# Seven block products for a third group of a dense layer, and steps of an attention moved around it

## The chip, the cores and the metric

The kernel runs on one core of one Trainium2 chip. The metric is device time in microseconds (us), measured several times; the kernel before has a median of 198.84 us. The five engines of the core work side by side and wait for each other through semaphores: TensorE (matmuls; PE in the profile, PEld for its weight loads), VectorE (DVE), ScalarE (ACT), GpSimd (POOL) and SyncE (SP), whose queue issues nearly all DMAs here. Each engine works through its own instructions in the order in which they were recorded. Matmul results lie in PSUM, eight banks of 128 x 512 fp32; everything else lies in SBUF.

## The reference

A linear attention with decay, in blocks of 64 tokens (batch 4, 8 heads, 768 tokens, head size 64), whose output goes into a dense layer, a gelu and a second dense layer (3072 tokens, 512 -> 2048 -> 512):

```python
for b in range(nb):
    qb, kb, vb = (q[:, :, sl], k[:, :, sl], v[:, :, sl])
    intra = np.einsum('bhic,bhjc->bhij', qb, kb) * Dmask[None]
    intra = np.einsum('bhij,bhjd->bhid', intra, vb)
    inter = np.einsum('bhid,bhde->bhie', qb * lam_pow[None], kv_state)
    out[:, :, sl] = intra + inter
    kb_dec = kb * rev_pow[None]
    kv_state = lam_block * kv_state + np.einsum('bhsd,bhse->bhde', kb_dec, vb)
x = attn_out.transpose(0, 2, 1, 3).reshape(B * S, H * D)
h = x @ w_in
g = 0.5 * h * (1.0 + np.tanh(c * (h + 0.044715 * h * h * h)))
return g @ w_out
```

## The kernel before

**Attention.** It is cut into 24 steps. Step n holds 256 tokens and 4 of the 8 heads; steps 2i and 2i + 1 make token block i. What a step needs: three loads of 256 KB (`load_step`, L60), the casts to fp16 (`cast_q` on VectorE, L282; `cast_k` on ScalarE, L295), a transpose of q and k by DMA on SyncE's queue (`transpose_dma`, L303, from step 8 on), the scaling of v on GpSimd (`scale_v`, L266), the scores (L350), their mask on VectorE (`causal`, L360), the key-value products (L385 or L450), the outputs (L399 and L408, or L436 and L461), the copy of the outputs into xT on ScalarE (`x_out`, L487), and twice the running state on VectorE (`update`, t at L503 and L506) with its spreading on GpSimd (u, L513). `R(n, s)` (L902) does scores of step n and outputs of step s; `burst(ns, ss)` (L415) does the same for two steps at once. `U(n)` is the second state update. `prep(s)` is casts, transpose and v, and also issues the loads of step s + 3.

**Dense layers.** The twelve token blocks make seven groups: `groups = [[0, 1], [2], [3], [4, 5], [6, 7], [8, 9], [10, 11]]`. When the last output of a group is copied, `queue_group(g)` (L544) puts the group's matmul pieces into a list, `filler`, and `fill(n)` (L898) takes the next n pieces from it, between the attention steps. The order on TensorE is therefore written out by hand, from L1060 on for the steps 13 to 23. Each piece is a closure that records its matmuls and what follows them on the other engines.

**First product, plain** (`mm1`, L557): for a group of 512 tokens 16 pieces of 4 matmuls of 512 columns (L561), each followed by a gelu on ScalarE (L565). Groups 0 to 4 use it.

**First product, by blocks** (`seven`, L726): groups 5 and 6, named in `SEVEN` (L531). The 2 x 2 block product over half the inner size, half the hidden size and half the tokens is done with seven products instead of eight, from four sums of blocks of w_in (`sum_win`, L144, on VectorE, made once, in tiles `ws`) and four sums of blocks of x (`sum_x`, L713, tiles `xs`). The hidden size is cut into four sets k. In a set each of the products m = 1 to 7 has 4 matmuls of 256 columns (L739), into banks X (two, in turn), W and Y. Product 1 opens X and is copied to SBUF by ScalarE (`copied("m1")`), 6 is added in the same bank and copied by VectorE (`"u2"`), 7 is added to that, then 4. Product 2 goes to W and VectorE adds the copy of 1. Product 5 opens Y and is copied by ScalarE (`"q"`), 3 is added in the same bank. VectorE adds the copies to the banks (`added`, L760), ScalarE then does the four gelus of the set (L756). The copies lie in tiles of the pool `ld`, which also holds the loads of q and k.

`merge` (L781) puts these pieces between the second product's pieces of the group before, which are still in `filler`: this is a mixed stretch. `SLOTS` says after which m one of the old pieces follows, `lead` how many old pieces stay in front of the mixed ones.

**Second product** (`product`, L616): for groups 1 to 6 also seven block products (m, and p for a half of the rows), with sums of w_out blocks made once and sums of the gelu output (`sum_g`, L602, tiles `gs`, VectorE). ScalarE copies (L657), VectorE adds (L677, L683, L686), and for the last quarter GpSimd (L692). `behind` hangs a `sum_g` on a piece. A group in front of one in `SEVEN` cuts its pieces in two halves.

Of the kernel before, what the change touches and what calls it, by code (L numbers as in the profile page):

```python
# [8 lines left out]
FP32 = mybir.dt.float32  # L9
FP16 = mybir.dt.float16  # L10
AF = mybir.ActivationFunctionType
ALU = mybir.AluOpType
# [3 lines left out]
def kernel(  # L16
# [10 lines left out]
    nc = tc.nc  # L27
# [32 lines left out]
    def load_step(s, names="qkv"):  # L60
        b, r = divmod(s, 2 * NSB)
        sb, half = divmod(r, 2)
        ts = ld32.setdefault(s, [])
        for nm, src in (("q", q), ("k", k), ("v", v)):
            if nm not in names:
                continue
            t = ld.tile([P, HH, 2, D], FP32, tag=nm + "32", name=f"{nm}32_{s}")
            rows = src[b, half * HH : (half + 1) * HH, sb * SB : (sb + 1) * SB, :]
            queue = nc.scalar if (nm, s) == ("v", 0) else nc.sync
            pin(queue.dma_start(out=t[:].rearrange("p h j d -> p h (j d)"),  # L70
                                in_=rows.rearrange("h (p j) d -> p h (j d)", j=2)))
            ts.append(t)
# [172 lines left out]
    def prep(s):  # L245
        prep_qk(s)
        prep_v(s)
# [21 lines left out]
    def prep_qk(s):  # L269
        cast_qk(s)  # L270
        transpose_dma(s)

    def cast_qk(s):
        cast_q(s)
        cast_k(s)
# [252 lines left out]
                                for i in range(2)]  # L528
        return gs_kept[1:]

    SEVEN = (5, 6)  # L531
    SLOTS = {5: {1: 0, 2: 1, 5: 1, 6: 1, 3: 1, 7: 1}, 4: {1: 0, 2: 1, 5: 0, 6: 1, 3: 1, 7: 1}}
    groups = [[0, 1], [2], [3], [4, 5], [6, 7], [8, 9], [10, 11]]
    group_of = {sb: (g, i) for g, sbs in enumerate(groups) for i, sb in enumerate(sbs)}
    filler = []
# [8 lines left out]
    def queue_group(g, lead=0, per_set=0):  # L544
# [177 lines left out]
        def release():  # L722
            while pending:
                pending.pop(0)()

        def seven(m, k):  # L726

            st = of_set.setdefault(k, {})
            for name in {1: "X", 2: "W", 5: "Y"}.get(m, ""):
                key = name + str(k % 2) if name == "X" else name  # L730
                if key not in hbank:
                    hbank[key] = ps_M.tile([P, 2, SB], FP32, tag="M", name="H" + name)
                st[name] = hbank[key]
            dst = st[{2: "W", 5: "Y", 3: "Y"}.get(m, "X")]
            a, b = X_FACTORS[m]
            for i in range(2):
                f = 2 * k + i
                for c in range(2):
                    pin(nc.tensor.matmul(  # L739
                        dst[:, i, :],  # L740
                        w_in_block(a, slice(c, c + 1), slice(f * P, f * P + P))[:, 0],
                        x_block(b, slice(c, c + 1))[:, 0],
                        start=(m in (1, 2, 5) and c == 0 and i == 0), stop=(m in (2, 3, 4) and c == 1),
                        skip_group_check=True))

            def copied(name, tag, eng):
                t = ld.tile([P, HH, 2, D], FP32, tag=tag, name=f"{name}_{g}_{k}")
                t = t[:].rearrange("p h j d -> p (h j d)").rearrange("p (i t) -> p i t", i=2)
                if eng is nc.scalar:
                    pin(nc.scalar.activation(out=t, in_=dst[:], func=AF.Copy))  # L750
                else:
                    pin(eng.tensor_copy(out=t, in_=dst[:]))
                st[name] = t

            def gelu(F, T, src):
                pin(nc.scalar.activation(out=gT[:, 2 * k : 2 * k + 2, F, T * SB : T * SB + SB],  # L756
                                         in_=src, func=AF.Gelu_apprx_tanh))

            def added(F, T, name):
                pin(nc.vector.tensor_tensor(st[name], dst[:], st[name], ALU.add))  # L760
                pending.append(lambda src=st[name]: gelu(F, T, src))

            if m == 1:
                copied("m1", "q32", nc.scalar)
            elif m == 2:
                added(0, 0, "m1")
            elif m == 5:
                copied("q", "q32", nc.scalar)
                release()
            elif m == 6:  # L770
                copied("u2", "k32", nc.vector)
            elif m == 3:
                added(0, 1, "u2")
            elif m == 7:
                added(1, 1, "q")
            elif m == 4:
                pending.insert(0, lambda: gelu(1, 0, dst[:]))
            if k == HF // 2 - 1 and m in (3, 7, 4):
                release()

        def merge(lead, per_set):  # L781

            old = filler[:]
            del filler[:]

            def h(n=1):
                for _ in range(min(n, len(old))):
                    filler.append(old.pop(0))

# [12 lines left out]
            h(lead + len(old) + 1 - 28 - 1 if len(old) >= 28 else lead - 1)  # L802
            sums = [1, 2, 4, 3]
            unread = {1: 16, 2: 12, 4: 8, 3: 4}
            slots = SLOTS[per_set]
            for k in range(HF // 2):
                for m in (1, 2, 5, 6, 3, 7):
                    filler.append(lambda m=m, k=k: seven(m, k))
                    if m == 2 and k > 0:
                        filler.append(lambda k=k: seven(4, k - 1))  # L810
                    while k >= 2 and sums and m == 7 and len(old) <= unread[sums[0]]:
                        also(sum_g, 0, 4, (sums.pop(0),))
                        if len(sums) == 2 and k == 2:
# [51 lines left out]
        if g in SEVEN:  # L865
            merge(lead, per_set)
            parts = (0, 1) if g + 1 in SEVEN else (None,)
            for m, p in order:
                for part in parts:
                    filler.append(lambda m=m, p=p, part=part: product(m, p, part))  # L870
            at = len(filler) - len(order) * len(parts)
            for k, m in enumerate((2, 4, 3)):
                behind(len(parts) * k, 4, 8, (m,))
            return
        for i in range(HF):
            for fs in ([[i, i + HF]] if per == 2 else [[i], [i + HF]]):
# [21 lines left out]
    def fill(n):  # L898
        for _ in range(min(n, len(filler))):
            filler.pop(0)()  # L900

    def R(n, s, ahead=None, keep=False):  # L902

        if n is not None:
            scores(n)
        if ahead:
            ahead()
        products(n, s)
        if n is not None:
            causal(n)  # L910
        if s is not None and s % 2 == 1:
            g, i = group_of[s // 2]
            if i == len(groups[g]) - 1 and g > 0:
                queue_group(g)
        if n is not None and not keep:
            update(n, 0)

    def U(n):
        update(n, 1)
# [138 lines left out]
            sum_win((n - 7) // 2, (n - 1) % 2, nc.vector)  # L1058

    cast_qk(16)  # L1060
    load_step(17, "qk")
    transpose_dma(16)
    load_step(17, "v")
# [13 lines left out]
    fill(1)  # L1077
    U(15)
    U(16)
    fill(8)  # L1080
    prep(18)
    R(17, 15)
    fill(1)
    U(17)
    fill(1)
    sum_win(3, 0, nc.vector)
    fill(2)
    prep(19)
    sum_win(3, 1, nc.vector)
    fill(2)  # L1090
    sum_win(4, 0, nc.vector)
    fill(2)
    sum_win(4, 1, nc.vector)
    fill(2)
    prep_qk(20)
    fill(1)
    prep_qk(21)
    prep_v(20)
    fill(3)

    burst((18, 19), (16, 17))
    prep_v(21)
    fill(2)
    U(18)
    U(19)
    fill(4)
    prep_qk(22)
    fill(2)
    burst((20, 21), (18, 19), 11, 4)
    fill(3)  # L1110
    U(20)
    U(21)
    fill(20)
# [39 lines left out]
```

## Time and profile before

| | |
|---|---|
| median of 3 runs | 198.84 us (198.83 to 198.92) |
| span of the profiled execution, first to last instruction | 197.1 us; a time of its own is not listed for it |
| TensorE busy | 191.5 us, granted clock 1.000 over the span |
| VectorE, ScalarE, GpSimd busy | 151.6, 122.2, 73.3 us |
| DMA moved | 38.13 MB, 193 GB/s in the mean |

Where the last groups stand on TensorE in the profiled execution (us from the start of the span):

| stretch | what TensorE does |
|---|---|
| 87.1 to 95.2 | burst of steps 13 and 14, first product of group 3, burst of 15 and 16 |
| 95.2 to 98.7 | rest of group 3's first product |
| 98.7 to 111.9 | group 3's second product, with step 17 at 103.1 |
| 111.9 to 129.2 | group 4's plain first product, with bursts of 18, 19 and of 20, 21 |
| 129.2 to 153.9 | group 4's second product, mixed with group 5's first from 134.0 |
| 153.9 to 160.3 | burst of 22, 23, last outputs |
| 160.3 to 181.4 | group 5's second product, mixed with group 6's first from 161.6 |
| 181.4 to 193.8 | group 6's second product |

How to read it: a row of the timeline has the start, the duration of the (merged) instructions, the engine, the line of the kernel, the operation, the output and inputs by name, the shape and the count; in brackets stands the idle time before it with what ended it. Durations of matmuls are modelled and overlap, so the pitch from start to start is used for them. The page's slices cut the span into 40 parts of 4.9 us; a digit is the busy share in tenths.

### The profile page before, as it was taken

How to read it: one execution, taken by the hardware profiler on the slowest of the kernel's cores; microseconds unless marked ns; L12 is line 12 of the kernel's file. 1: busy time of each engine (PE TensorE's matmuls, PEld its weight loads, DVE VectorE, ACT ScalarE, POOL GpSimd, SP SyncE). 2: the span in 40 equal slices, each digit the busy share in tenths (PEclk: the TensorE clock that was granted, in tenths of full speed). 3: DMA queues.
4: the chain of work that ended last, by engine and by line, in shares of the span. 5: the costliest groups of instructions: out<-in, count | busy, mean ns of one | idle time of the engine just before them, and what ended most of it. 6: DMA issues, size and time to landing. Idle time of an engine off the chain costs nothing.

```text
span 197.1 us, 5915 instructions
## 1 busy us (share of the span) xinstructions
PE 191.5 (97%) x2431; PEld 140.0 (71%) x2431; DVE 151.6 (77%) x297; ACT 122.2 (62%) x249; POOL 73.3 (37%) x85
## 2 busy tenths in 40 slices
PE   8979999999999999999999999999999999999993
PEld 2556544446888888654688764588888888888882
DVE  4797622789999889849999937998668996588620
ACT  3673878357874685686835378844768845779221
POOL 6594123456554841068854517165002030002000
PEclk9999999999999999999999999999999999999999
DMA  6999999999999999999997998400220300030205
GB/s 172 290 324 384 387 387 388 299 287 292 236 216 225 259 343 220 213 266 247 271 268 149 268 328 213 88 4 0 53 85 25 109 6 0 0 110 0 106 19 197
DMA packets 62810, 38.13 MB, mean 193 GB/s; under 512 B 18624, under 2 KB 55744, under 8 KB 62784
## 3 DMA queue, kind: packets, MB, share of 16 engines
q1 hardware_dynamic: 62240, 37.50, 75.0%
q8 instruction: 19, 0.31, 0.6%
q10 hardware_dynamic: 544, 0.26, 0.5%
q14 instruction: 7, 0.06, 0.1%
HBM read 27.26 MB, written 6.29 MB: 170 GB/s over the span
## 4 chain that ended last, share of the span: by engine, by line
PE 89%; SPq 4%; DMA 4%; ACT 0%; issue 0%
PE Hps L561 25%; PE MX L640 18%; PE MY L640 9%; PE HX L739 7%; PE O2ps L576 7%; PE MW L640 4%; DMA wi<-in_moe_w_in_dram 4%; SPq L70 4%; PE HY L739 4%; PE S L350 3%; PE Hps L830 3%; PE HW L739 2%; PE OK L408 2%; PE O L461 1%; PE O L436 1%; PE OK L399 1%
## 5 line engine op out<-in xcount | busy, mean ns | idle before, releaser
L561 PE MATMUL Hps<-xT,w_in 128*128 128x512 f16 (+1 forms) x288 | 50.5, 332 | 0.0
L513 POOL TENSOR_TENSOR u<-t,lumask 128x256 f16<-128x256 f32 x40 | 30.9, 787 | 39.5 <-DVE t L506 25.8
L561 PEld LDWEIGHTS <-w_in 128*128 128x128 f16 x288 | 27.9, 98 | 19.1
L565 ACT ACTIVATE gT<-Hps 128x512 f16<-128x512 f32 x56 | 33.3, 597 | 11.3 <-PE Hps L561 10.8
L360 DVE TENSOR_TENSOR PT<-S,mask 128x512 f16<-128x512 f32 x48 | 30.3, 681 | 7.5 <-PE S L350 7.5
L266 POOL TENSOR_TENSOR v<-v,dv 128x512 f16<-128x512 f32 x24 | 27.7, 1156 | 18.2 <-DMA v<-in_v_dram 14.2
L640 PEld LDWEIGHTS <-gs 128*128 128x128 f16 x320 | 31.2, 98 | 3.6
L640 PEld LDWEIGHTS <-gT 128*128 128x128 f16 x240 | 23.3, 98 | 3.2 <-ACT gT L565 0.2
L640 PE MATMUL MX<-w_sum,gs 128*128 128x256 f16 x160 | 21.4, 273 | 0.0
L282 DVE TENSOR_TENSOR qk<-q,dq 128x512 f16<-128x512 f32 x23 | 18.4, 802 | 1.7 <-DMA q<-in_q_dram 1.7
L692 POOL TENSOR_TENSOR o<-u,q 128x512 f32<-128x512 f32 (+1 forms) x5 | 6.3, 1253 | 35.2 <-ACT u L657 35.2
L295 ACT ACTIVATE qk<-k 128x512 f16<-128x512 f32 x23 | 14.4, 625 | 7.4 <-DMA k<-in_k_dram 7.2
L610 DVE TENSOR_TENSOR gs<-gT 128x1024 f16<-128x1024 f16 (+1 forms) x24 | 16.9, 711 | 1.6 <-ACT gT L565 1.6
L576 PE MATMUL O2ps<-w_out,gT 128*128 128x512 f16 x64 | 14.6, 379 | 0.0
L487 ACT ACTIVATE xT<-OK 128x256 f16<-128x256 f32 x26 | 9.9, 452 | 6.7 <-PE OK L408 6.2
L739 PEld LDWEIGHTS <-ws 128*128 128x128 f16 x128 | 12.5, 97 | 1.8
L657 ACT ACTIVATE u<-MX 128x256 f32<-128x256 f32 x18 | 6.9, 384 | 10.1 <-PE MX L640 10.1
L487 ACT ACTIVATE xT<-O 128x256 f16<-128x256 f32 x22 | 8.0, 459 | 5.3 <-PE O L461 4.5
L576 PEld LDWEIGHTS <-gT 128*128 128x128 f16 x64 | 6.1, 98 | 6.6
L640 PE MATMUL MY<-w_out,gs 128*128 128x256 f16 x80 | 10.7, 273 | 0.0
L350 PEld LDWEIGHTS <-qkT 64*64 64x64 f16 x384 | 6.0, 106 | 6.6 <-issue 3.6
L640 PE MATMUL MX<-w_sum,gT 128*128 128x256 f16 x80 | 10.4, 273 | 0.0
(96 smaller groups left out, 317.3 us busy)
## 6 DMA issues: line engine op xcount, KB each, us to landing
q<-in_q_dram SPq DMA_DIRECT2D x24, 256.0 KB, 5.1
k<-in_k_dram SPq DMA_DIRECT2D x24, 256.0 KB, 5.1
v<-in_v_dram SPq DMA_DIRECT2D x23, 256.0 KB, 5.4
out_dram<-o SPq DMA_DIRECT2D x23, 256.0 KB, 4.2
wo<-in_moe_w_out_dram SPq DMA_DIRECT2D x4, 1024.0 KB, 9.5
wi<-in_moe_w_in_dram SPq DMA_DIRECT2D x4, 512.0 KB, 8.0
wi<-in_moe_w_in_dram SPq DMA_DIRECT2D x2, 1024.0 KB, 12.7
v<-in_v_dram ACTq DMA_DIRECT2D x1, 256.0 KB, 4.2
```

Of the source, the lines that this page charges most:

```text
L266: pin(nc.gpsimd.tensor_tensor(wide(tv[:]), ld32[s][2][:], decay(dv, s), ALU.mult))
L282: pin(q_eng.tensor_tensor(wide(tq), q32[:], decay(dq, s), ALU.mult))
L295: pin(nc.scalar.activation(out=wide(tk), in_=k32[:], func=AF.Copy))
L360: pin(nc.vector.tensor_tensor(t[:, hl].rearrange("p b c d -> p b (c d)"), Sps[:].rearrange("p b c d -> p b (c d)"), mask[:].unsqueeze(1).t ...
L487: pin(nc.scalar.activation(out=d, in_=o, func=AF.Copy))
L513: pin(nc.gpsimd.tensor_tensor(u[:], state[half][:].unsqueeze(2).to_broadcast([P, 2, 2, D]), lumask[:, 2 * half : 2 * half + 2, :].unsqueez ...
L561: pin(nc.tensor.matmul(by_block(Hps[:, i, :]), w_in16[:, c, f * P : (f + 1) * P], x(c), start=(c == 0), stop=(c == NC - 1)))
L565: pin(nc.scalar.activation(out=dst, in_=Hps[:], func=AF.Gelu_apprx_tanh))
L576: pin(nc.tensor.matmul(O2[tau][0][:], gT[:, f % HF, f // HF, tau * P : (tau + 1) * P], w_out16[:, f, :], start=(n == 0), stop=(n == NF - 1)))
L610: pin(nc.vector.tensor_tensor(g_rows(m, i), g_rows(a, i), g_rows(b, i), op))
L640: pin(nc.tensor.matmul(dst, lhsT, rhs, start=(opens and i == 0), stop=(closes and i == HF - 1), skip_group_check=True))
L739: pin(nc.tensor.matmul(dst[:, i, :], w_in_block(a, slice(c, c + 1), slice(f * P, f * P + P))[:, 0], x_block(b, slice(c, c + 1))[:, 0], sta ...
```

## The change

Group 4, the fifth, joins `SEVEN`. Its first product is then done by seven block products in four sets and mixed with group 3's second product, whose pieces are halved for it. Within a set the order becomes 1, 5, (4 of the set before), 2, 6, 3, 7. From the second set on, product 1 is no longer copied to SBUF: ScalarE copies it from its bank into bank W, and product 2 accumulates on it there; the gelu reads W, and VectorE's add of 1 and 2 is left only in a group's first set. The scratch copies move from the pool `ld` into halves of w_in16 and w_out16 that are no longer read. The sums of w_in are made earlier. Step 17 goes ahead of group 3's second product; steps 18 to 20 come after the first mixed stretch and 21 to 23 after the second; step 20 and step 23 become single steps, 21 and 22 a burst.

```diff
-    SEVEN = (5, 6)
-    SLOTS = {5: {1: 0, 2: 1, 5: 1, 6: 1, 3: 1, 7: 1}, 4: {1: 0, 2: 1, 5: 0, 6: 1, 3: 1, 7: 1}}
+    SEVEN = (4, 5, 6)
+    SLOTS = {5: {1: 0, 5: 1, 2: 1, 6: 1, 3: 1, 7: 1}, 4: {1: 0, 5: 1, 2: 0, 6: 1, 3: 1, 7: 1}}
...
+        def held(name, i):
+
+            if name == "q":
+                t = w_in16[:, i, DFF // 2 : DFF].bitcast(FP32)
+                return t.rearrange("p (i a t) -> p i a t", i=2, a=2)
+            t = w_out16[:, 4 * i : 4 * i + 4, HE : 2 * HE].bitcast(FP32)
+            return t.rearrange("p (i a) t -> p i a t", a=2)
...
-            for name in {1: "X", 2: "W", 5: "Y"}.get(m, ""):
+            for name in {1: "X" if k == 0 else "XW", 2: "W", 5: "Y"}.get(m, ""):
...
-                        start=(m in (1, 2, 5) and c == 0 and i == 0), stop=(m in (2, 3, 4) and c == 1),
+                        start=((m in (1, 5) or (m, k) == (2, 0)) and c == 0 and i == 0),
+                        stop=(m in (2, 3, 4) and c == 1),
...
-            if m == 1:
-                copied("m1", "q32", nc.scalar)
+            if m == 1 and k == 0:
+                copied("m1", nc.scalar)
+            elif m == 1:
+                pin(nc.scalar.activation(out=st["W"][:], in_=dst[:], func=AF.Copy))
+            elif m == 2 and k == 0:
+                added(0, 0, "m1")
             elif m == 2:
-                added(0, 0, "m1")
+                pending.append(lambda: gelu(0, 0, quarters(dst[:])))
             elif m == 5:
-                copied("q", "q32", nc.scalar)
+                copied("q", nc.scalar)
                 release()
             elif m == 6:
-                copied("u2", "k32", nc.vector)
+                copied("u2", nc.vector)
+                release()
...
-                for m in (1, 2, 5, 6, 3, 7):
+                for m in (1, 5, 2, 6, 3, 7):
                     filler.append(lambda m=m, k=k: seven(m, k))
-                    if m == 2 and k > 0:
+                    if m == 5 and k > 0:
                         filler.append(lambda k=k: seven(4, k - 1))
...
-            for k, m in enumerate((2, 4, 3)):
-                behind(len(parts) * k, 4, 8, (m,))
+            for k, m in zip((8, 10, 12) if g + 1 in SEVEN else (0, 1, 2), (2, 4, 3)):
+                behind(k, 4, 8, (m,))
...
     cast_qk(16)
+    sum_win(3, 0, nc.vector)
+    sum_win(3, 1, nc.vector)
     load_step(17, "qk")
...
     U(15)
     U(16)
-    fill(8)
+    fill(3)
+    R(17, 15, mix=(10, 4))
+    fill(4)
+    U(17)
+    fill(4)
+    sum_win(4, 0, nc.vector)
     prep(18)
-    R(17, 15)
...
+    fill(12)
+    sum_win(4, 1, nc.vector)
+    prep(19)
+    fill(12)
+    prep(20)
+    fill(12)
+    prep_qk(21)
+    fill(12)
+
+    burst((18, 19), (16, 17))
     fill(1)
...
+    U(18)
+    U(19)
     fill(3)
+    R(20, 18)
     prep_v(21)
     fill(2)
-    U(18)
-    U(19)
-    fill(4)
+    R(None, 19, mix=(5, 4))
+    U(20)
+    fill(14)
     prep_qk(22)
-    fill(2)
-    burst((20, 21), (18, 19), 11, 4)
...
+    fill(12)
     prep_qk(23)
-    fill(23)
+    fill(10)
     prep_v(22)
     prep_v(23)
-    fill(13)
-    burst((22, 23), (20, 21))
+    fill(14)
+    burst((21, 22), (20,))
+    fill(1)
+    U(21)
     U(22)
-    U(23)
-    fill(8)
+    fill(3)
+    R(23, 21)
+    fill(4)
     burst((), (22, 23), 3, 4)
     fill(len(filler))
```

`R` hands `mix` on to `queue_group` as `lead` and `per_set`; `quarters` only reshapes an access.

More of the change, by code (lines that the diff above doesn't have):

```diff
@@ L724, in release, with quarters @@
                 pending.pop(0)()
+        def quarters(t):
+            return t.rearrange("p i (a t) -> p i a t", a=2)
+        def held(name, i):
[4 more added lines that the diff above has]
+            return t.rearrange("p (i a) t -> p i a t", a=2)
         def seven(m, k):
             st = of_set.setdefault(k, {})
-            for name in {1: "X", 2: "W", 5: "Y"}.get(m, ""):
+            for name in {1: "X" if k == 0 else "XW", 2: "W", 5: "Y"}.get(m, ""):
                 key = name + str(k % 2) if name == "X" else name
@@ L742, in seven, with copied @@
                         x_block(b, slice(c, c + 1))[:, 0],
-                        start=(m in (1, 2, 5) and c == 0 and i == 0), stop=(m in (2, 3, 4) and c == 1),
+                        start=((m in (1, 5) or (m, k) == (2, 0)) and c == 0 and i == 0),
+                        stop=(m in (2, 3, 4) and c == 1),
                         skip_group_check=True))
-            def copied(name, tag, eng):
-                t = ld.tile([P, HH, 2, D], FP32, tag=tag, name=f"{name}_{g}_{k}")
-                t = t[:].rearrange("p h j d -> p (h j d)").rearrange("p (i t) -> p i t", i=2)
+            def copied(name, eng):
+                st[name] = t = held(name, 1 if name == "m1" else k % 2)
@@ L749, in copied @@
                 if eng is nc.scalar:
-                    pin(nc.scalar.activation(out=t, in_=dst[:], func=AF.Copy))
+                    pin(nc.scalar.activation(out=t, in_=quarters(dst[:]), func=AF.Copy))
                 else:
-                    pin(eng.tensor_copy(out=t, in_=dst[:]))
-                st[name] = t
+                    pin(eng.tensor_copy(out=t, in_=quarters(dst[:])))
             def gelu(F, T, src):
-                pin(nc.scalar.activation(out=gT[:, 2 * k : 2 * k + 2, F, T * SB : T * SB + SB],
-                                         in_=src, func=AF.Gelu_apprx_tanh))
+                to = gT[:, 2 * k : 2 * k + 2, F, T * SB : T * SB + SB]
@@ L759, in added @@
+                pin(nc.scalar.activation(out=quarters(to), in_=src, func=AF.Gelu_apprx_tanh))
             def added(F, T, name):
-                pin(nc.vector.tensor_tensor(st[name], dst[:], st[name], ALU.add))
+                pin(nc.vector.tensor_tensor(st[name], quarters(dst[:]), st[name], ALU.add))
                 pending.append(lambda src=st[name]: gelu(F, T, src))
-            if m == 1:
-                copied("m1", "q32", nc.scalar)
+            if m == 1 and k == 0:
[4 more added lines that the diff above has]
+                added(0, 0, "m1")
@@ L776, in seven @@
             elif m == 4:
-                pending.insert(0, lambda: gelu(1, 0, dst[:]))
+                pending.insert(0, lambda: gelu(1, 0, quarters(dst[:])))
             if k == HF // 2 - 1 and m in (3, 7, 4):
@@ L900, in fill, with R @@
             filler.pop(0)()
-    def R(n, s, ahead=None, keep=False):
+    def R(n, s, ahead=None, keep=False, mix=()):
         if n is not None:
@@ L913, in R @@
             if i == len(groups[g]) - 1 and g > 0:
-                queue_group(g)
+                queue_group(g, *mix)
         if n is not None and not keep:
@@ L1079 @@
     U(16)
-    fill(8)
-    prep(18)
-    R(17, 15)
-    fill(1)
-    U(17)
-    fill(1)
-    sum_win(3, 0, nc.vector)
-    fill(2)
[L1088 to L1098, printed above, removed]
+    fill(3)
[4 more added lines that the diff above has]
+    sum_win(4, 0, nc.vector)
+    prep(18)
+    fill(12)
[7 more added lines that the diff above has]
+    burst((18, 19), (16, 17))
+    fill(1)
+    U(18)
+    U(19)
     fill(3)
-    burst((18, 19), (16, 17))
+    R(20, 18)
     prep_v(21)
     fill(2)
-    U(18)
-    U(19)
-    fill(4)
+    R(None, 19, mix=(5, 4))
+    U(20)
+    fill(14)
     prep_qk(22)
-    fill(2)
-    burst((20, 21), (18, 19), 11, 4)
[L1110 to L1113, printed above, removed]
+    fill(12)
     prep_qk(23)
-    fill(23)
+    fill(10)
     prep_v(22)
     prep_v(23)
-    fill(13)
-    burst((22, 23), (20, 21))
+    fill(14)
+    burst((21, 22), (20,))
+    fill(1)
+    U(21)
     U(22)
-    U(23)
-    fill(8)
+    fill(3)
+    R(23, 21)
+    fill(4)
     burst((), (22, 23), 3, 4)
```

## The prediction

> **What bounds the kernel now.** First the page: engine totals, the slices, the chain of waits.
>
> ```profile
> PE 191.5 (97%) x2431; PEld 140.0 (71%) x2431; DVE 151.6 (77%) x297; ACT 122.2 (62%) x249; POOL 73.3 (37%) x85
> ...
> PE   8979999999999999999999999999999999999993
> ...
> DVE  4797622789999889849999937998668996588620
> ...
> PE 89%; SPq 4%; DMA 4%; ACT 0%; issue 0%
> ```
>
> TensorE runs without a hole from 20 us to the tail, and the chain is TensorE. So a matmul taken away is gained whole, and a wait put in front of TensorE is paid whole. The page cannot tell which waits are near. For that I read the timeline of TensorE, whose starts give the pitch:
>
> ```profile
> 95.21 3.62 PE L561 MATMUL Hps<-xT,w_in 128*128 128x512 f16 x16
> 98.66 1.91 PE L640 MATMUL MX<-w_out,gT 128*128 128x256 f16 x16
> ...
> 103.12 0.42 PE L350 MATMUL S<-qkT 64*64 64x128 f16 x16
> ...
> 104.05 1.04 PE L640 MATMUL MY<-w_sum,gs 128*128 128x256 f16 x8
> ...
> 118.05 7.07 PE L561 MATMUL Hps<-xT,w_in 128*128 128x512 f16 x32
> 125.05 0.64 PE L350 MATMUL S<-qkT 64*64 64x128 f16 x32
> ...
> 130.92 1.91 PE L640 MATMUL MW<-w_out,gT 128*128 128x256 f16 x16
> 132.67 1.47 PE L640 MATMUL MY<-w_sum,gs 128*128 128x256 f16 x12
> ```
>
> 32 matmuls of 512 columns take 7.00 us (219 ns each), 16 of 256 take 1.75 us (109 ns, half). Step 17 (103.12 to 104.05) is 0.93 us, behind four first-product pieces (95.21 to 98.66) and ten block products. Next the SyncE row that transposes step 17's q and k, and that tile's time from issue to landing:
>
> ```profile
> 94.84 1.84 SPq L303 DMA_TRANSPOSE qkT<-qk  x1
> ...
> DMA to landing us min/median/max: 5.3/5.3/5.3
> ```
>
> It lands at 94.84 + 5.3 = 100.1 us, 3 us before it is needed. Last VectorE beside GpSimd:
>
> ```profile
> 105.97 0.68 DVE L151 TENSOR_TENSOR ws<-w_in 128x1024 f16<-128x1024 f16 x1
> 106.57 1.10 DVE L282 TENSOR_TENSOR qk<-q,dq 128x512 f16<-128x512 f32 x1
> 107.59 1.53 DVE L151 TENSOR_TENSOR ws<-w_in 128x1024 f16<-128x1024 f16 x1
> ...
> 106.22 0.91 POOL L513 TENSOR_TENSOR u<-t,lumask 128x256 f16<-128x256 f32 x1 [4.10 <-DVE t L506]
> 107.08 1.49 POOL L266 TENSOR_TENSOR v<-v,dv 128x512 f16<-128x512 f32 x1
> ...
> 129.52 0.65 DVE L718 TENSOR_TENSOR xs<-xT,xs 128x512 f16<-128x512 f16 x1
> 130.43 0.41 DVE L718 TENSOR_TENSOR xs<-xT,xs 128x512 f16<-128x512 f16 x1
> ```
>
> VectorE operations with two SBUF inputs and GpSimd operations take turns. u ends at 106.22 + 0.91 = 107.13 and qk 0.54 later; v ends at 108.57, 0.90 after qk, and ws 0.55 after v. So a turn costs 0.55 for gs, ws and qk, 0.28 for xs (130.17, 0.28 after a u at 129.89), 0.47 for u, 0.90 for v. With one input in PSUM (the masks at L360, L506) there is no such wait: 0.68 beside GpSimd too. VectorE is full from 99 to 112 us and nothing on TensorE waits for it there. That cover is what the change removes.
>
> **The change part by part.**
>
> A. The fifth group's first product: 64 matmuls of 512 go (64 x 0.219 = 14.0 us), 112 of 256 come (4 sets x 7 x 4, x 0.109 = 12.25): -1.75 us. The Trainium skill ("TensorE: Matmul & The Clock Gate", Back-to-back issue gap) speaks against this: weight load and matmul together set the spacing, 131 ns at 512 columns and 81 ns at 128. By it, estimated, 64 x 131 = 8.4 us would become 9.1 to 14.7 us, a loss of 0.7 to 6.3. This trace disagrees (219 and 109, loads of 98 ns hidden), and its rows decide.
>
> B. Step 17 moves ahead of the ten products. Four first-product pieces end at 95.21 + 3.5 = 98.7, and the scores then need the transpose of 100.1. Its queue is unchanged up to there (loads of step 18 are in front in both). TensorE waits 1.4 us. What hid the landing was the 4.4 us of block products.
>
> C. Fifth group's mixed stretch. Step 17 runs from 100.1 to 101.1; 40 product matmuls (4.4) bring the first block product (m=1) to 105.5. Pieces of 0.44 follow: 3 is the seventh (108.1) and needs the fourth w_in sum; 7 is the ninth (109.0) and needs product 6 copied. VectorE: masks from 100.6 (scores + 0.46, as 79.99 to 80.45), 2 x 0.60, state 0.39: 102.2. Then, in its order: gs, four xs, gs, o, gs, ws, qk, the add of 1 and 2, the copy of 6. GpSimd has u of step 17, then v of 18, 19 and 20, and nothing holds these back but loads that landed or land by 105.7. Taking turns: gs 102.8, u 103.3, xs 103.6, v 104.5, xs 104.8, v 105.7, xs 106.0, v 106.9, xs 107.15, gs 107.7, o 108.3, gs 108.9, ws 109.5, qk 110.1, add 110.7, copy 111.35 (0.60 each alone). So 3 waits until 109.55 (1.45), and 7, now due at 110.4, until 111.4 (1.0): +2.4. Without the turns (xs 0.34, others 0.60) ws ends at 106.6 and the copy at 108.7: 0. I take 2.4, by the rows above. Later sets carry 2.4 to 4.3 us of VectorE work in 4.8: no wait.
>
> D. Sixth group. From the start of burst (18,19): TensorE burst 1.73 (116.32 to 118.05), 16 products 1.75, step 20 0.82, half of W 0.87, step 19's output 0.45, W 0.87, twelve products 1.31: first block product at 7.8; product 6's second half of the old group at 10.9, seventh block product at 11.3. VectorE: masks from 0.9 (behind the last gs), 6 x 0.60, copies 0.4, states 8 x 0.195 and gaps: 6.45. Then u (20), v (21), u, v (22), v (23) alternate with the xs: xs end at 10.1, o 10.7, gs 11.55, gs 12.15, add 12.85, copy 13.5. The old product waits 0.75 for gs, and 7, due at 12.05, until 13.5: +2.2. Without turns 0.
>
> E. Seventh group. Burst (21,22) is 1.2 us instead of 1.7 to 1.9, and the bank of the next product is freed by the first mask of step 21, some 1.9 after the burst's start (155.10 + 0.68 - 153.94 = 1.84 before): 0.7. Step 21's u (state, then 0.61 on GpSimd) ends 0.3 late for step 23: +1.0 (0 to 1.2).
>
> F. Product 1 on a copy. In 9 sets ScalarE copies 1 from PSUM to PSUM, and 2 waits for it; 9 adds (0.69) leave VectorE. Three pieces (1.31 us) lie between the end of 1 and the start of 2; delay 0.2 + copy 0.60 (the L750 row) leaves 0.5 spare. A copy into PSUM is not in this trace: bounds 0.38 (256 columns at L657) and 1.2 (twice L750, also the slowest row for 512 columns doubled). At 1.2 it would cost 0.1 x 9 = 1. I take 0.60, cost 0. Scratch in unused weight halves costs 0: same copies, the weights' last readers are done when group 4 is finished.
>
> G. Moved pieces. Attention counts the same matmuls: before 0.93 + 1.73 + 1.53 + 1.8 + 1.03 = 7.0 (step 17, three bursts, last outputs), after 0.93 + 1.73 + 0.82 + 0.45 + 1.2 + 0.9 + 1.0 = 7.0: 0. Both halves of the third w_in sum (2 x 0.68) go into VectorE's 2.06 us gap before 87.5; the following masks start 0.15 late and the wait for GpSimd until 91.59 takes that up: 0, or 0.2 without that wait. Loads 21 to 23 on SyncE now stand behind transposes 18 to 20, whose casts come some 9 to 15 us later; landing 5 to 6 us after issue they are still over 5 us early: 0. Stores and the tail keep order: 0.
>
> Sum: -1.75 + 1.4 + 2.4 + 2.2 + 1.0 = +5.25 us. On the profiled span, 197.1 + 5.25 = 202.4. The runs' median 198.84 lies 1.7 above the span (launch and end, unchanged), so 204.1 us. What a measurement tells from no change is 0.2%, 0.4 us.
>
> **The rivals.**
>
> R1, the turns cost little: GpSimd's v operations fall outside the xs windows, or the copies come just in time. For it: without turns C and D are 0 by 0.3 us. Against: nothing in GpSimd's order delays them, and at 100.63 v started at once. Then -1.75 + 1.4 + 0 to 1.0: 198.5 to 199.5, in the middle 199.0 us.
>
> R2, the other side, faster: VectorE in time, and the transpose of step 17 lands by 98.7, as it does if it takes the 3.9 us of light traffic instead of 5.3. It decides at a landing of 3.9 us or less. For it: transposes from 104.6 on took 3.0 to 3.3. Against: three 256 KB loads are in the queue before it, in both. Then 198.84 - 1.75 = 197.1 us.
>
> R3, a new ScalarE wait: the PSUM copy or its queue is late by more than 0.5 us in most of 9 sets. ScalarE is busy for 14.7 of 20 us in such a stretch before, so there is room, but it serves in order. At 0.4 us each +3.6: 207.7 us.
>
> That seven products replace sixteen is sure from the instruction list (48 more matmuls); that the change doesn't do what it says is no rival.
>
> **How the numbers follow.** Forecast 0.68, R1 0.15, R2 0.10, R3 0.07. The range 199.2 to 206.0 holds the forecast with D or E halved or C larger by half, and half of R1; it leaves out R2, the other half of R1, and R3: about 0.2. Its low end is far below because C and D each may be 0. Faster (below 198.44): R2, 0.10, and a little of R1: 0.11. Same: half of R1, 0.08. Slower: 0.81.
>
> **What would show it.** A: 112 block-product rows for the fifth group, 0.44 us per four where nothing waits. B: a hole of about 1.4 us before step 17's scores, ended by the DMA of qkT. C: holes before the fifth group's first products 3 and 7, ended by VectorE's ws and its copy, with v rows of 1.2 to 1.5 us between xs rows of 0.6 to 1.2. D: the same two kinds at the sixth group. E: under 1.2 us around steps 21 to 23. F: no hole in front of product 2 ended by ScalarE. Wrong if TensorE is whole through 100 to 112 us, or if the holes stand in later sets.

## The result, and the profile after

The changed kernel takes 204.38 us (204.25 to 204.62, 4 runs) where the kernel before takes 198.88 us in the same comparison (198.83 to 198.95, 4 runs): ratio 1.0265, 95% interval 1.0242 to 1.0287. The profiled span grew from 197.1 to 202.5 us.

The page of the changed kernel, engine totals, TensorE's slices and the chain of waits:

```profile
PE 191.4 (95%) x2479; PEld 144.3 (71%) x2479; DVE 157.8 (78%) x308; ACT 124.7 (62%) x257; POOL 70.8 (35%) x85
...
PE   8979999999999999999896999996999999999993
...
PE 71%; DVE 14%; DMA 6%; SPq 4%; issue 2%; ACT 1%; POOL 0%; DVEq 0%
```

TensorE has 48 more matmuls and is busy as long as before (191.4 us against 191.5). The row of slices (a fortieth of the span each, 5.06 us) has dents where it had none: an 8 (96 to 101 us), a 6 (106 to 111) and a 6 (137 to 142). The chain is no longer TensorE alone: VectorE holds 14% of it, a DMA 2% more than before.

TensorE's timeline shows the dents one by one (start, length, line, tile, number of matmuls; in brackets the idle time in front and what ended it). The edit moved lines: L750 are now the block products, L763 the copy of product 6, L770 the adds, L767 the gelus, L778 the copy of product 1 from bank to bank.

```profile
95.25 3.62 PE L561 MATMUL Hps<-xT,w_in 128*128 128x512 f16 x16
99.64 0.42 PE L350 MATMUL S<-qkT 64*64 64x128 f16 x16 [0.77 <-DMA qkT<-qk]
...
107.12 0.60 PE L640 MATMUL MY<-w_sum,gs 128*128 128x256 f16 x4
108.72 0.61 PE L750 MATMUL HY<-xT,ws 128*128 128x256 f16 x4 [1.00 <-DVE ws L151]
109.17 0.60 PE L640 MATMUL MX<-w_sum,gs 128*128 128x256 f16 x4
110.52 0.60 PE L750 MATMUL HX<-xs,ws 128*128 128x256 f16 x4 [0.75 <-DVE w_out L763]
...
128.59 0.62 PE L461 MATMUL O<-qkT,u 128*128 128x128 f16 x8
129.38 1.91 PE L640 MATMUL MX<-w_out,gT 128*128 128x256 f16 x16 [0.17 <-DVE PT L360]
...
138.50 0.60 PE L750 MATMUL HY<-xT,ws 128*128 128x256 f16 x4
139.52 0.61 PE L640 MATMUL MX<-w_sum,gs 128*128 128x256 f16 x4 [0.42 <-DVE gs L610]
141.44 0.60 PE L750 MATMUL HX<-xs,ws 128*128 128x256 f16 x4 [1.31 <-DVE w_out L763]
```

Four matmuls of 256 columns start 0.44 us after the four before them, so what a start lies above that is the hole: 108.72 - 107.12 - 0.44 = 1.16 us for product 3 (due when the fourth w_in sum is ready) and 0.91 for product 7 (when 6 is copied). In the sixth group it is 0.58 for a product of the old group, which reads a gs sum, and 1.48 for product 7. In front of step 17's scores it is 99.64 - 95.25 - 16 x 0.219 = 0.89 us, ended by the transpose, and behind the burst (18,19), where eight matmuls of 128 columns take 8 x 0.055, it is 0.35 for the first product, ended by a mask.

### The profile page after: what moved, and what is told of

Same layout as the page of the kernel before. It is cut to its first block, busy times and chain, and to the rows that moved or that the text cites. A ratio compares the mean times of both kernels' runs of the same rounds, so it can differ in the third digit from the quotient of the medians.

```text
span 202.5 us, 6043 instructions
## 1 busy us (share of the span) xinstructions
PE 191.4 (95%) x2479; PEld 144.3 (71%) x2479; DVE 157.8 (78%) x308; ACT 124.7 (62%) x257; POOL 70.8 (35%) x85
## 4 chain that ended last, share of the span: by engine, by line
PE 71%; DVE 14%; DMA 6%; SPq 4%; issue 2%; ACT 1%; POOL 0%; DVEq 0%
PE Hps L561 15%; PE MX L640 13%; PE HX L750 9%; PE MY L640 7%; PE O2ps L576 7%; PE HY L750 4%; DMA wi<-in_moe_w_in_dram 4%; SPq L70 4%; DVE gs L610 4%; DVE PT L360 3%; DVE xs L718 3%; PE Hps L847 3%; PE MW L640 3%; DMA qkT<-qk 2%; PE HW L750 2%; PE S L350 2%
## 5 line engine op out<-in xcount | busy, mean ns | idle before, releaser
L513 POOL TENSOR_TENSOR u<-t,lumask 128x256 f16<-128x256 f32 x40 | 29.6, 756 | 31.1 <-DVE t L506 23.1
L561 PE MATMUL Hps<-xT,w_in 128*128 128x256 f16 (+1 forms) x224 | 36.2, 318 | 0.0
L561 PEld LDWEIGHTS <-w_in 128*128 128x128 f16 x224 | 21.7, 98 | 12.2
L565 ACT ACTIVATE gT<-Hps 128x512 f16<-128x512 f32 x40 | 23.9, 597 | 9.2 <-PE Hps L561 8.8
L640 PEld LDWEIGHTS <-gT 128*128 128x128 f16 x240 | 23.1, 98 | 3.3 <-issue 0.6
L750 PEld LDWEIGHTS <-ws 128*128 128x128 f16 x192 | 18.7, 98 | 5.8 <-issue 2.4
L487 ACT ACTIVATE xT<-OK 128x256 f16<-128x256 f32 x32 | 12.2, 454 | 6.9 <-PE OK L408 5.3
L750 PE MATMUL HX<-xs,ws 128*128 128x256 f16 x96 | 14.4, 272 | 2.1 <-DVE w_out L763 2.1
L763 DVE COPY w_out<-HX 128x512 f32<-128x512 f32 x12 | 8.3, 688 | 9.3 <-ACT gT L767 7.0
L750 PEld LDWEIGHTS <-w_in 128*128 128x128 f16 x144 | 14.1, 98 | 2.0
L767 ACT ACTIVATE gT<-w_out 128x512 f16<-128x512 f32 x15 | 9.5, 631 | 7.2 <-DVE w_out L770 7.2
```

The lines of the kernel that those rows point to most:

```text
L487: pin(nc.scalar.activation(out=d, in_=o, func=AF.Copy))
L513: pin(nc.gpsimd.tensor_tensor(u[:], state[half][:].unsqueeze(2).to_broadcast([P, 2, 2, D]), lumask[:, 2 * half : 2 * half + 2, :].unsqueez ...
L561: pin(nc.tensor.matmul(by_block(Hps[:, i, :]), w_in16[:, c, f * P : (f + 1) * P], x(c), start=(c == 0), stop=(c == NC - 1)))
L565: pin(nc.scalar.activation(out=dst, in_=Hps[:], func=AF.Gelu_apprx_tanh))
L640: pin(nc.tensor.matmul(dst, lhsT, rhs, start=(opens and i == 0), stop=(closes and i == HF - 1), skip_group_check=True))
L750: pin(nc.tensor.matmul(dst[:, i, :], w_in_block(a, slice(c, c + 1), slice(f * P, f * P + P))[:, 0], x_block(b, slice(c, c + 1))[:, 0], sta ...
```

## The experiments

All kernels start from the changed one unless it is said otherwise. The kernel before took 198.93 to 199.05 us beside them. A "hole" is what a row's start lies above TensorE's pitch.

**The v's of steps 18 to 20 by VectorE.** This takes GpSimd out of the stretch in which VectorE is late.

```diff
-    def scale_v(s):
+    def scale_v(s, eng=nc.gpsimd):
...
     sum_win(4, 0, nc.vector)
-    prep(18)
+    prep_qk(18)
     fill(12)
     sum_win(4, 1, nc.vector)
+    prep_v(18, nc.vector)
```

and so for 19 and 20.

> The changed kernel with the v's of steps 18, 19 and 20 scaled by VectorE instead of GpSimd, each one gap of twelve pieces later. Theory (the turns between VectorE and GpSimd make VectorE late): VectorE's own list is unchanged up to the copy of product 6, GpSimd has only u of step 17 beside it; the xs go back to 0.34 us each, ws ends near 106.5 us instead of 108.6 and the copy near 108.3 instead of 110.4, so the holes of 1.16 and 0.91 us in front of products 3 and 7 of the fifth group fall to 0 to 0.3 in sum: 202.3 to 202.7 us. Rival (VectorE has too much of its own work there, the turns cost little): at least 1.5 us of the two holes stays, 203.8 us or more. Second rival (the three v's, 0.6 us each, only move the wait on VectorE to a later set): the two holes go, others come after 113 us, 203.5 to 204.5 us.

202.58 us (201.91 to 203.78), ratio 1.0182 (1.0143 to 1.0222). VectorE in the changed kernel, and GpSimd beside it:

```profile
102.29 0.83 DVE L718 TENSOR_TENSOR xs<-xT 128x512 f16<-128x512 f16 x1
103.23 1.08 DVE L718 TENSOR_TENSOR xs<-xT,xs 128x512 f16<-128x512 f16 x1
104.23 1.26 DVE L718 TENSOR_TENSOR xs<-xT 128x512 f16<-128x512 f16 x1
105.41 0.41 DVE L718 TENSOR_TENSOR xs<-xT,xs 128x512 f16<-128x512 f16 x1
...
106.95 1.11 DVE L610 TENSOR_TENSOR gs<-gT,gs 128x1024 f16<-128x1024 f16 x1
107.99 0.68 DVE L151 TENSOR_TENSOR ws<-w_in,ws 128x1024 f16<-128x1024 f16 x1
...
101.94 0.90 POOL L513 TENSOR_TENSOR u<-t,lumask 128x256 f16<-128x256 f32 x1 [1.48 <-DVE t L506]
102.81 2.40 POOL L266 TENSOR_TENSOR v<-v,dv 128x512 f16<-128x512 f32 x2
106.47 1.04 POOL L266 TENSOR_TENSOR v<-v,dv 128x512 f16<-128x512 f32 x1 [1.26 <-DMA v<-in_v_dram]
```

VectorE in the experiment, and TensorE's products 3 and 7:

```profile
102.26 0.84 DVE L718 TENSOR_TENSOR xs<-xT 128x512 f16<-128x512 f16 x1
103.20 0.43 DVE L718 TENSOR_TENSOR xs<-xT,xs 128x512 f16<-128x512 f16 x1
103.54 0.42 DVE L718 TENSOR_TENSOR xs<-xT 128x512 f16<-128x512 f16 x1
...
105.41 0.68 DVE L610 TENSOR_TENSOR gs<-gT,gs 128x1024 f16<-128x1024 f16 x1
106.01 0.69 DVE L151 TENSOR_TENSOR ws<-w_in,ws 128x1024 f16<-128x1024 f16 x1
...
110.81 0.69 DVE L266 TENSOR_TENSOR v<-v,dv 128x512 f16<-128x512 f32 x1
...
107.09 0.60 PE L640 MATMUL MY<-w_sum,gs 128*128 128x256 f16 x4
107.53 0.60 PE L750 MATMUL HY<-xT,ws 128*128 128x256 f16 x4
107.96 0.60 PE L640 MATMUL MX<-w_sum,gs 128*128 128x256 f16 x4
108.55 0.60 PE L750 MATMUL HX<-xs,ws 128*128 128x256 f16 x4
```

VectorE has the same operations up to the copy of 6, in the same order and from the same start. Without GpSimd's v's the two xs that met one are shorter by 0.65 and 0.84 us and the gs beside the third v by 0.43, ws ends 2.0 us earlier, and the holes of 1.16 and 0.91 us become 0 and 0.15. None came later instead. The turns are the cause, and VectorE's own load is not. A v costs VectorE 0.69 us where GpSimd takes 1.0 to 1.5.

**The v's of 21 to 23 alone.** The same in the sixth group.

```diff
     R(20, 18)
-    prep_v(21)
     fill(2)
...
     fill(14)
+    prep_v(21, nc.vector)
     prep_qk(22)
...
-    prep_v(22)
-    prep_v(23)
+    prep_v(22, nc.vector)
+    prep_v(23, nc.vector)
```

> The changed kernel with the v's of steps 21, 22 and 23 alone scaled by VectorE instead of GpSimd, that of 21 fourteen pieces later, those of 22 and 23 where they are recorded. Theory (the turns make VectorE late in the sixth group too): the xs take 0.34 us each except beside a u, and the holes of 0.58 us (product of the old group, for gs) and 1.47 us (product 7, for the copy of 6) fall to 0 to 0.3 us in sum, with the fifth group's holes as they were: 202.4 to 202.9 us. Rival (VectorE is late there by its own masks, states and sums): 1.5 us or more of the two holes stays, 203.9 us or more. Second rival (three more operations of 0.6 us on VectorE move the wait to the masks of steps 21 and 22): holes between 140 and 160 us, 203.0 to 204.4 us.

202.45 us (202.24 to 202.82), ratio 1.0168 (1.0150 to 1.0186). The holes of the sixth group fall to 0 and 0.12 us, those of the fifth stand at 1.19 and 0.91. The first theory holds.

**The loads of step 18 behind the transpose of step 17.**

```diff
-    load_ahead(18)
     fill(5)
     burst((15, 16), (13, 14), ahead=lambda: (prep_qk(17), scale_v(17)))
+    load_ahead(18)
```

> The changed kernel with the three loads of step 18 recorded behind the transpose of step 17 instead of in front of it. Theory (the transpose is late because 768 KB are in the queue in front): it lands in 3.0 to 4.0 us instead of 4.7 and the hole in front of step 17's scores falls from 1.0 to 0.3 us or less; VectorE was idle for only 0.33 us in front of the masks of step 17, so up to 0.7 of it comes back in front of products 3 and 7: 203.4 to 204.2 us. Rival (the transpose is late by its issue alone, behind the cast of q): it still lands in 4.7 us, the hole stays at 1.0 us, 204.4 us. Second rival (the loads of step 18, now later, are themselves late for the cast of q of step 18): a hole from that load, over 204.8 us.

203.36 us (203.29 to 203.72), ratio 1.0218 (1.0200 to 1.0237). The transpose is issued at 94.9 us as before. Its tile's view in the changed kernel, issue to landing:

```profile
DMA to landing us min/median/max: 4.7/4.7/4.7
```

and in the experiment:

```profile
DMA to landing us min/median/max: 3.1/3.1/3.1
```

The scores start without a hole. What stood in front in the queue set the landing. The time lies 0.04 us below the expected range: I had 0.7 us coming back in front of products 3 and 7, but product 3's hole fell as well (1.16 to 0.84), since the later loads kept a v away from VectorE.

**The copy of product 6 on ScalarE.** Only for the first set of each group.

```diff
-                copied("u2", nc.vector)
+                copied("u2", nc.scalar if k == 0 else nc.vector)
```

> The changed kernel with the copy of product 6 of the first set of each of the last three groups on ScalarE instead of VectorE. Theory (product 7 waits only because the copy stands at the end of VectorE's late queue): the hole in front of product 7 falls from 0.91 to 0.2 us or less in the fifth group and from 1.47 to 0.2 or less in the sixth, the holes for ws and gs stay, and 0.3 to 0.8 us come back behind in front of product 5 of the next set, whose bank VectorE's add of product 3 frees: 202.6 to 203.2 us. Rival (VectorE's lateness is paid in full one step later, at that add): 204.0 to 204.6 us. Second rival (ScalarE is no earlier, its queue being full of gelus and copies): the holes stay and are ended by ScalarE, 204.4 us or more.

203.12 us (202.88 to 203.52), ratio 1.0205 (1.0184 to 1.0226). Product 7 waits no more, those for ws and gs stay (1.19, 0.58), and product 5 of the second set now waits for VectorE's add:

```profile
140.17 0.60 PE L750 MATMUL HX<-xT,w_in 128*128 128x256 f16 x4
141.38 0.60 PE L750 MATMUL HY<-xs,ws 128*128 128x256 f16 x4 [0.60 <-DVE w_out L770]
```

The holes in front of product 7 were 2.4 us together (0.91 and 1.48), and 1.26 us are won. So half of what the copy held up is VectorE's lateness itself and comes back one step on.

**Product 1 accumulated on a copy, alone.** The kernel before with this part only, in the sixth and seventh group: six copies by ScalarE instead of six adds by VectorE, and the new order of products.

```diff
-            if m == 1:
+            if m == 1 and k == 0:
                 copied("m1", "q32", nc.scalar)
-            elif m == 2:
+            elif m == 1:
+                pin(nc.scalar.activation(out=st["W"][:], in_=dst[:], func=AF.Copy))
+            elif m == 2 and k == 0:
                 added(0, 0, "m1")
+            elif m == 2:
+                pending.append(lambda: gelu(0, 0, dst[:]))
...
-                for m in (1, 2, 5, 6, 3, 7):
+                for m in (1, 5, 2, 6, 3, 7):
```

> The kernel before with one part of the change alone: in the sixth and seventh group ScalarE copies product 1 from bank to bank in sets 2 to 4, product 2 is accumulated on the copy, and the products run 1, 5, 2, 6, 3, 7. Theory (the copy takes about 0.6 us, three pieces of 0.44 lie in front of product 2): no hole on TensorE, 198.5 to 199.3 us. Rival (the copy into a bank is slow or stands in ScalarE's queue, 0.4 us in each of 6 sets): 201.3 us, with holes in front of product 2 ended by ScalarE. Second rival (six adds taken from VectorE end waits that TensorE has now): below 198.4 us.

198.85 us (198.73 to 199.51, 10 runs), ratio 0.9995 (0.9984 to 1.0006): no difference. The group of copies (L767 in this kernel, where the block products are L739) has

```profile
L767 ACT ACTIVATE HW<-HX 128x512 f32<-128x512 f32 x6 | 3.5, 582 | 6.4 <-PE HX L739 6.4
```

0.582 us each, and TensorE waits for none. The adds taken from VectorE won nothing, as TensorE did not wait for them either.

**The edits together.** First the three that gained alone: v's of 18 to 23, and the loads.

> The three single edits together: the v's of 18 to 23 on VectorE, and the loads of step 18 behind the transpose of step 17. Theory (the landing and the two late stretches are all but about 1.4 us of what the change costs): the gains add up, 204.4 - 1.9 (fifth group) - 1.0 (transpose) - 1.9 (sixth group) = 199.6, 199.2 to 199.9 us, with holes left only around steps 18 to 20 (0.4 to 0.6 us) and 21 to 23 (0.8 us). Rival (the gains overlap, since TensorE that comes earlier meets a VectorE that does not): a new hole of over 0.5 us in the mixed stretches, 200.4 us or more. Second rival (the moved attention of part G is dearer than written, and only the holes hid it): holes as in the theory, but 200.4 us or more.

200.09 us (200.04 to 200.20), ratio 1.0053 (1.0041 to 1.0065), 0.2 us above the expected range. The gains nearly add up, but a hole of 0.57 us for product 7 in the fifth group is new: TensorE that is earlier meets the copy at the end of VectorE's list. Around the bursts 0.60 and 0.40 us stay:

```profile
126.27 0.62 PE L461 MATMUL O<-qkT,u 128*128 128x128 f16 x8
127.31 1.91 PE L640 MATMUL MX<-w_out,gT 128*128 128x256 f16 x16 [0.41 <-DVE PT L360]
...
125.37 1.28 DVE L610 TENSOR_TENSOR gs<-gT 128x1024 f16<-128x1024 f16 x2
126.57 2.47 DVE L360 TENSOR_TENSOR PT<-S,mask 128x512 f16<-128x512 f32 x4
```

Here a burst holds all eight banks and the first mask frees one; on VectorE the masks stand behind the gs sums that the last mixed piece records. So the last of these sums goes behind them, to the fourth piece of the old group's products:

```diff
-            also(sum_g, 0, 4, sums)
-            also(sum_g, 4, 8, (1,))
+            if g + 1 not in SEVEN:
+                also(sum_g, 0, 4, sums)
+                also(sum_g, 4, 8, (1,))
+            return sums
...
+            if g + 1 in SEVEN:
+                behind(3, 0, 4, sums)
+                behind(3, 4, 8, (1,))
```

> The three edits together, and the last three gs sums of a mixed stretch recorded behind the masks of the burst that follows (with the fourth piece of the old group's products) instead of in front of them. Theory (the burst uses all eight banks, the next product waits for the first mask, and the masks stand behind these sums): the holes in front of the first product after the bursts (0.4 to 0.6 us each) fall to 0.2 us or less: 198.5 to 199.2 us. Rival (the sums are then late for the old group's product that reads them, or hold up the masks of step 20): a hole ended by gs or PT of the same size, 199.5 us or more. Second rival (the holes come from the burst's length, not from the sums): holes as they were, same time as the three edits within 0.2 us.

199.81 us (199.69 to 200.41), ratio 1.0043 (1.0028 to 1.0058): a partial miss. Both holes behind the bursts go, but the sum now stands in front of step 20's masks and a bank is late there, 0.6 us; in front of product 7 of the fifth group 0.62 us stay. The next kernel moves the sum to the sixth piece, behind those masks, and the cast of q of step 18 four pieces back.

```diff
-                behind(3, 0, 4, sums)
-                behind(3, 4, 8, (1,))
+                behind(5, 0, 4, sums)
+                behind(5, 4, 8, (1,))
...
-    prep_qk(18)
-    fill(12)
+    fill(4)
+    prep_qk(18)
+    fill(8)
```

> The three edits together, the last gs sum of a mixed stretch recorded with the sixth piece of the old group's products (behind the masks of the step after the burst, so that no mask stands behind it), and the cast of q of step 18 four pieces later (so that the copy of product 6 comes 0.6 us earlier). Theory (each remaining hole is VectorE's order): of the holes of 0.62, 0.57 and 0.42 us with the sum at the fourth piece the first falls to 0.1 or less, the second to 0.2 or less, the third stays at 0.2 to 0.4: 199.81 - 0.9 = 198.9, 198.6 to 199.2 us, the time before. Rival (the sum is now late for the old group's product 5): a hole in front of it of 0.5 us or more, 199.4 us or more.

199.20 us (199.01 to 200.47, 11 runs), ratio 1.0022 (1.0008 to 1.0036). The moved sum did what it should: no hole above 0.2 us is left around the steps. The moved cast did nothing: four pieces later it still stands in front of the add on VectorE, so product 7's hole stays at 0.56 us, and the sixth group's is 0.51. Last, the copy of 6 on ScalarE besides:

> The same with the copy of product 6 of the first set on ScalarE besides. Theory (product 7 then waits for nothing on VectorE): the hole in the sixth group goes too, 198.4 to 198.9 us, faster than the kernel before by 0 to 0.4 us; what is left against the 1.85 us of matmul time saved is one more small attention step (0.4) and holes of 0.2 at the starts of steps. Rival (ScalarE's queue is late for the copy, or the wait reappears at the bank of product 5 of the second set as it did with the copy moved alone): holes of 0.4 us or more in one of the two groups, no faster than the five edits.

197.89 us (197.88 to 198.02, 5 runs), ratio 0.9948 (0.9934 to 0.9961): faster than the kernel before by 1.1 us. Its page:

```profile
PE 190.2 (97%) x2479; PEld 144.7 (74%) x2479; DVE 155.3 (79%) x311; ACT 126.2 (64%) x260; POOL 64.5 (33%) x79
...
PE   8979999999999999999999999999999999999993
...
PE 89%; SPq 4%; DMA 4%; ACT 0%; issue 0%
```

It has the 2479 matmuls of the changed kernel, and the slices and the chain of the kernel before. It beat its own expectation by 0.5 us: the copy was worth 1.3 us, more than the two holes (1.07) that were in sight.

**Two of them taken back.** Is each cause one by itself, in a kernel with slack elsewhere? The first undoes both edits of the v's in the kernel of six (`prep(18)` whole, where its cast of q now stands), the second the edit of the loads.

> The kernel of the six edits with one of them taken back: the v's of steps 18 to 23 on GpSimd again, where the changed kernel records them. Theory (the turns are a cause by themselves, whatever the order on VectorE): xs rows of 0.8 to 1.3 us again, a hole of about 0.8 us for ws in the fifth group and holes of 0.5 to 0.8 us for gs or an add in the sixth: 197.9 + 2.0 = 199.9, 199.3 to 200.6 us. Rival (copy, sum and cast in their new places leave VectorE slack enough for the turns): 198.5 us or less.

201.04 us (200.19 to 202.29), ratio 1.0105 (1.0066 to 1.0144), above the expected range. In the fifth group only 0.6 us of holes return, because the v's of 19 and 20 wait there for their later loads (GpSimd is idle for 3.3 and 1.2 us in front of them). In the sixth they are larger than expected, 0.85 for gs and 0.77 for an add:

```profile
137.21 0.61 PE L640 MATMUL MX<-w_sum,gs 128*128 128x256 f16 x4 [0.69 <-DVE gs L610]
...
139.73 0.60 PE L750 MATMUL HY<-xs,ws 128*128 128x256 f16 x4 [0.60 <-DVE w_out L770]
```

> The kernel of the six edits with another taken back: the three loads of step 18 in front of the transpose of step 17 again. Theory (the landing costs by itself what the profile shows): the transpose lands 4.6 to 4.7 us after its issue, a hole of 0.8 to 1.0 us in front of step 17's scores and none behind it: 198.6 to 198.9 us. Rival (a late step 17 makes VectorE late for the mixed stretch again): further holes of 0.3 us or more between 105 and 112 us, 199.1 us or more.

199.34 us, ratio 0.9999 (0.9979 to 1.0019), above the expected range and in the rival's. Nine of the ten runs lie between 198.60 and 199.94, the four fastest at 198.60 to 198.70, the tenth at 203.02. The time decides little, the profile more: landing after 4.9 us, one hole of 1.06 us in front of step 17 (100.68 - 96.12 - 16 x 0.219), nothing behind it up to 150 us.

```profile
96.12 3.62 PE L561 MATMUL Hps<-xT,w_in 128*128 128x512 f16 x16
100.68 0.42 PE L350 MATMUL S<-qkT 64*64 64x128 f16 x16 [0.94 <-DMA qkT<-qk]
```

That a late step 17 does not pass its lateness on, once VectorE has slack, is shown by it. Against the kernel of six edits this execution has lost another 0.9 us before 96 us; its granted clock reads 0.50 from 15 to 18 us.

## Why the prediction was right, and where its terms were off

The kernel of six edits runs the changed kernel's matmuls with next to no hole, so it splits the result in two. Giving each TensorE row the time to the next row's start, from 60 us on, and summing by line:

| part | predicted, us | measured, us | from |
|---|---|---|---|
| A block products for 512-column ones | -1.75 | -1.65 | six edits - before: L561 -13.90, block products +12.25 |
| G attention regrouped | 0 | +0.57 | six edits - before: lines 350 to 461, 13.53 to 14.10 |
| B landing of step 17's transpose | +1.4 | +0.84 | changed - six edits, in front of step 17 |
| C fifth group | +2.4 | +2.07 | 1.16 + 0.91 |
| D sixth group | +2.2 | +2.06 | 0.58 + 1.48 |
| E steps 21 to 23 | +1.0 | +0.51 | changed - six edits: 0.37 behind burst (21,22), 0.14 in step 23 |
| not listed: burst (18,19) to step 20 | | +0.55 | changed - six edits: 0.33 behind the burst, 0.22 in step 20 |
| F copy of product 1 | 0 | 0 | copy alone: 0.9995 |

Measured, these come to +4.95; small differences in other lines and a tail 0.2 us longer make the +5.3 us of the span. Predicted were +5.25. That the sum came so near is partly luck: B, C, D and E were put 1.5 us too high together, and A, G and the waits that were not listed 1.2 us too low.

A, C, D and F held as mechanisms and, within 0.35 us, in size. The prediction's two holes stand where it put them, in C in front of 3 and 7, in D in front of an old product and 7, and the experiments with the v's remove them and nothing else. Rival R1 (the turns cost little) falls with that, R3 (ScalarE late) with the copy alone, R2 (transpose in 3.9 us) with the 4.7 us of the profile; R2's mechanism, though, is the one that the moved loads brought about. One detail of C differs: the third v waited for its load until 106.47 us and met a gs, not an xs.

B was mis-sized: I took 5.3 us from issue to landing, as the kernel before had it, and it was 4.7. One trace's figure was taken for fixed: with the three loads in front, the same transpose took 4.4 to 5.3 us in the seven profiles that have them. The direction of its cause, the loads in front, was argued and is now shown (3.1 without them).

G was wrong at zero. The same attention matmuls take 0.57 us more in the new grouping, with no wait behind it in the profile. Stretch by stretch the profile of six edits shows where: burst (21,22) takes 1.50 us (152.17 to 153.67), and G and E wrote 1.2; step 23 takes 1.01 instead of 0.9; and the burst (22,23) of the kernel before took 1.72 (153.94 to 155.66), where G wrote 1.8. In burst (21,22) the 24 key-value products take 0.57 us up to the next row, the 32 of burst (18,19) 0.35:

```profile
125.26 0.42 PE L450 MATMUL K<-v,qk 64*64 64x64 f16 x32
125.61 0.62 PE L461 MATMUL O<-qkT,u 128*128 128x128 f16 x8
...
152.86 0.64 PE L450 MATMUL K<-v,qk 64*64 64x64 f16 x24
153.43 0.40 PE L461 MATMUL O<-qkT,u 128*128 128x128 f16 x4
```

Why fewer of them take longer is not shown. The same length is what E had wrong. In the changed kernel the bank came 1.87 us after the burst's start (157.81 to 159.68), as E had it (1.9), but with 1.50 us of burst in front of it TensorE waits 0.37 us and not 0.7. So one error stands in G and in E with opposite signs, and in the sum the two nearly cancel.

What the prediction missed is that in the sixth group, too, the first product behind the burst needs the bank that a mask frees, and that these masks stand behind the gs sums; it put "masks from 0.9 (behind the last gs)" into VectorE's list and did not ask which bank the next product gets, though it had named the same wait for E.

The Trainium skill ("SBUF — State Buffer", section "SBUF: two separate sides") has the turns as an exclusive lock: a VectorE operation with two SBUF inputs and a GpSimd operation that reads SBUF block each other for a whole instruction. The rows above agree: xs of 0.43 us grow to 1.08 and 1.26 beside v, and masks, with one input in PSUM, stay at 0.68 beside GpSimd, as the prediction read.

## What to carry to other kernels

A matmul saving is worth what the other engines' lists allow at their new due times: write out, for the stretch that gets denser, the order of each helper engine with the start of each operation, and look for the first one that TensorE then meets. Where VectorE's list is tight, count each GpSimd operation that falls beside its two-SBUF-input operations, and give GpSimd's work to VectorE (0.69 us instead of 1.0 to 1.5 and a turn) at a place with slack. A late operation at the end of a list has several causes in a row; removing one shows the next, so the gains of single edits don't simply add, and the last edit can be worth more than its own hole.

## What the runs showed of the hardware that was not expected

The queued DMA transpose of step 17's q and k took 3.0 to 3.4 us from issue to landing in the six profiles with no load just in front of it, and 4.4 to 5.3 in the seven with 768 KB of loads issued just before it.

The granted clock of TensorE can fall for some microseconds in the middle of a run. In the profile of the first experiment, stretches of 5 us (TensorE busy, PEld, VectorE, ScalarE, GpSimd, clock, DMA share, GB/s):

```profile
140.00:145.00 5.00, 5.00 (x33) 3.77 (x32) 1.92 (x5) 3.33 (x8) 0.00 (x0) 0.66 0.30 56
145.00:150.00 5.00, 5.00 (x49) 4.47 (x47) 3.56 (x6) 3.42 (x7) 0.00 (x0) 1.00 0.17 32
```

33 matmuls instead of 49 were issued at a clock of 0.66: about 1.6 us (the span of that execution is 202.0 us, of the experiment's three others 200.1 to 200.9). The profiles of the experiment with the v's of 21 to 23 and of the last one show the like at 15 to 18 us, with a clock of 0.50; the other ten read 1.00 from 10 to 190 us. Nothing in the traces says why.
